# A tile's eight transposes in one PSUM tile of two banks, with one copy, one cast and one subtraction

## The chip, the cores and the metric

The kernel runs on one core of a Trainium2 chip. The metric is the device time of one execution in microseconds. The core has five engines with a queue of instructions each: TensorE (PE in the profile; its weight loads are PEld), ScalarE (ACT), VectorE (DVE), GpSimd (POOL), and SyncE (SP), which here issues all DMAs. Each engine works through its own list in order and waits at an instruction until what that needs is there.

## What is computed

The reference is attention in a window of 64 positions, then two dense layers with an activation between them, twice over (2304 tokens, 512 features):

```
scores = where(mask, (q @ k.T) / sqrt(64), -1e9)        # 4 x 8 heads, 576 positions, head size 64
attn = exp(scores - max); attn = attn / (sum(attn) + 1e-9)
x = (attn @ v), heads side by side                       # 2304 x 512
h = x @ w_in                                             # 512 -> 1024
solu = h * softmax(h)
ln = (solu - mean) / sqrt(var + 1e-6) * g_ln
x2 = ln @ w_out                                          # 1024 -> 512
h = x2 @ w_in2                                           # 512 -> 2048
g = (a0 + a1 h + a2 h^2 + a3 h^3) / (1 + |b0| |h| + |b1| h^2 + 1e-6)
out = g @ w_out2                                         # 2048 -> 512
```

The weights come in double precision, and the products of the dense layers are made of three passes over split operands (high times high, high times low, low times high).

## The kernel before

The 2304 tokens are 18 tiles of 128. The first part of the program takes each tile through attention and the first layer: scores (`s`, L412 and L418), maximum, eight exponentials (`P`, L433), the sum, the normalisation on POOL in two halves (L446), the transposes of the eight 128x128 blocks of `P` (`pt`, L452), their copy to SBUF (`PT`, a helper's line, L316 on ACT or L318 on DVE), attention (`pv`, L472), the copy and the split of its result (`xh`, `xl`), the product with w_in (`h`, L577 for tiles 0 and 1 in plain fp32, L583 to L585 for the others in three passes), maximum, exponential and product of the activation (L591, `e` L595, L600), the layer norm, the transposes of its eight blocks (`pl`, L643), their cast to the high part (`lh`, L316) and the subtraction that gives the low part (`ll`, a helper's line, L312). After every third tile there are four blocks of 24 matmuls with w_out (`x`, L661 to L663). In between, ACT and DVE convert the weights of both layers from double precision (`xi`, `co`, `cc`; L524 to L562), and SP loads them. The second part, from about 300 us on, is the second layer (`hp`, L869 to L871, and `o`, L933 to L935) and has nothing to do with the change.

The transposes go to PSUM tiles of 128x512 fp32, one bank each, from a pool with two buffers under one tag. So one tile's eight transposes are two steps of four (`probs0`, `probs1`; `lnT0`, `lnT1`), each with a copy, or with a cast and a subtraction, of its own; and the four steps of a tile share the two buffers.

What sets the order is a planner (`class Schedule`). Each step is declared with its engine, a duration, the steps that it needs, the buffers that it takes and gives back (`RINGS`), and, for some, a due time (`WANT`). `latest` works due times backwards; `arrange` goes forward in time, and on the engine that is free first takes, of what can start by then, the step with the earliest due time. A table `SHIFT` of over 500 numbers, one for each kind of step, is added to the due times. The program is written out in the order that comes out of this, so each engine's list is fixed when the kernel is built. An h step of a tile needs h's single PSUM buffer, which the product (`solu_mul`, L600) of the tile before gives back.

Of the kernel before, what the change touches and what calls it, by code (L numbers as in the profile page):

```python
# [10 lines left out]
F32 = mybir.dt.float32  # L11
# [17 lines left out]
class Schedule:  # L29
# [131 lines left out]
WANT = {"scores": -14.41, "probs0": -5.07, "probs1": -11.61, "attend": -3.5, "h": 0.0, "lnT0": 18.0, "lnT1": 6.24,  # L161
# [8 lines left out]
    "zeros.0": 1.38, "load_q.0": 6.55, "load_k.0": -28.63, "load_v0.0": 141.12, "load_v1.0": -6.38,  # L170
    "scores.0": -20.87, "max.0": -45.99, "max_scale.0": -4.27, "exp00.0": -66.76, "exp01.0": 3.38, "exp02.0": -5.62,
    "exp03.0": -8.85, "exp10.0": 72.56, "exp11.0": -8.26, "exp12.0": -26.72, "exp13.0": -0.04, "rcp.0": 8.87,
    "norm0.0": 8.54, "norm1.0": 14.81, "probs0.0": 1.34, "probs_copy0.0": -62.03, "probs1.0": -5.85,
    "probs_copy1.0": 18.56, "attend.0": -46.92, "att_hi.0": -12.2, "h0.0": -269.2, "h1.0": 8.67, "h2.0": 3.37,
    "h3.0": 26.22, "solu_max.0": 31.19, "solu_exp.0": 2.85, "solu_mul.0": 11.29, "ln_square.0": -13.95,
    "ln_eps.0": -1.23, "ln_var.0": -50.09, "ln_root.0": 40.62, "ln_newton.0": 40.57, "ln_apply.0": 11.2,
    "lnT0.0": 10.64, "ln_lo0.0": -9.07, "lnT1.0": 26.11, "ln_hi1.0": 49.09, "ln_lo1.0": -7.2, "load_q.1": -15.97,
    "load_k.1": -1.82, "load_v0.1": -24.72, "load_v1.1": -50.83, "scores.1": 25.01, "max_scale.1": 44.65,
    "exp00.1": 3.81, "exp01.1": -10.95, "exp02.1": -8.5, "exp03.1": 0.02, "exp10.1": 44.36, "exp11.1": -14.96,
    "exp12.1": -41.69, "exp13.1": -29.73, "sum.1": -36.73, "rcp.1": 12.45, "norm0.1": -6.86, "norm1.1": -0.75,  # L180
    "probs0.1": -13.21, "probs_copy0.1": -14.32, "probs1.1": 54.09, "attend.1": -31.41, "att_hi.1": 44.51,
    "h0.1": 123.3, "h1.1": -79.07, "h2.1": -8.64, "h3.1": 8.6, "solu_max.1": 1.31, "solu_exp.1": 53.25,
    "solu_mul.1": -102.82, "ln_square.1": -111.94, "ln_eps.1": -5.47, "ln_var.1": 10.19, "ln_root.1": 23.16,
    "ln_newton.1": -19.91, "ln_apply.1": 1.34, "lnT0.1": -250.52, "ln_hi0.1": 42.1, "ln_lo0.1": 3.68,
    "lnT1.1": -90.22, "ln_hi1.1": -0.19, "ln_lo1.1": 0.09, "load_q.2": -53.75, "load_k.2": 2.2, "load_v0.2": 31.73,
    "load_v1.2": 31.01, "scores.2": 4.8, "max.2": 13.85, "max_scale.2": -3.04, "exp00.2": 3.57, "exp01.2": -9.12,
    "exp02.2": -64.47, "exp03.2": -59.28, "exp10.2": 55.78, "exp11.2": -5.48, "exp12.2": -62.63, "exp13.2": 4.22,
    "sum.2": -29.63, "norm0.2": -3.19, "norm1.2": -68.31, "probs0.2": -22.28, "probs_copy0.2": -58.18,
    "probs1.2": 27.82, "probs_copy1.2": 1.45, "attend.2": 54.95, "att_hi.2": 43.76, "att_lo.2": 3.12, "h0.2": 24.95,
    "h1.2": 5.79, "h2.2": 13.56, "h3.2": -33.94, "solu_exp.2": 19.34, "solu_mul.2": 19.14, "ln_square.2": 4.55,  # L190
    "ln_eps.2": -23.38, "ln_var.2": -2.95, "ln_root.2": 253.93, "ln_newton.2": -41.92, "ln_apply.2": -8.79,
    "lnT0.2": 73.62, "ln_hi0.2": 5.39, "ln_lo0.2": 72.68, "lnT1.2": -108.76, "ln_hi1.2": -115.31, "ln_lo1.2": 5.48,
    "x2_0.2": 30.09, "x2_out0.2": 0.27, "x2_1.2": -30.14, "x2_out1.2": -8.97, "x2_2.2": 31.15, "x2_out2.2": -8.93,
    "x2_3.2": -28.94, "x2_out3.2": 9.66, "x2_store.2": 36.3, "load_q.3": 55.5, "load_k.3": -61.69, "load_v0.3": 50.44,
    "load_v1.3": -21.04, "scores.3": 45.91, "max.3": 19.14, "max_scale.3": -27.79, "exp01.3": -57.15,
    "exp02.3": -13.57, "exp03.3": 14.11, "exp10.3": -27.25, "exp11.3": -86.72, "exp12.3": 14.24, "exp13.3": -17.77,
    "sum.3": 16.89, "norm0.3": 67.01, "norm1.3": 10.6, "probs0.3": 48.4, "probs_copy0.3": 14.82, "probs1.3": 46.89,
    "probs_copy1.3": -68.76, "attend.3": -12.43, "att_hi.3": 9.62, "att_lo.3": -2.23, "h0.3": -28.18, "h1.3": 4.45,
    "h2.3": 71.47, "h3.3": -17.32, "solu_max.3": 0.55, "solu_exp.3": -37.61, "solu_mul.3": 7.39,
    "ln_square.3": -13.89, "ln_eps.3": -8.0, "ln_var.3": -24.56, "ln_root.3": -42.0, "ln_newton.3": 18.28,  # L200
    "ln_apply.3": -34.59, "lnT0.3": -21.97, "ln_hi0.3": 2.92, "ln_lo0.3": 53.87, "lnT1.3": -44.68, "ln_hi1.3": 45.82,
    "ln_lo1.3": 55.16, "load_q.4": -0.97, "load_k.4": 79.18, "load_v0.4": 6.74, "load_v1.4": -37.63,
    "scores.4": -50.82, "max.4": -232.11, "max_scale.4": 7.78, "exp00.4": -72.47, "exp01.4": 66.42, "exp02.4": -2.95,
    "exp03.4": -55.86, "exp10.4": -3.36, "exp11.4": -9.42, "exp12.4": 98.46, "exp13.4": -13.13, "sum.4": -2.13,
# [64 lines left out]
FIRST = 2  # L269
# [817 lines left out]
```

## Time and profile before

| | |
|---|---|
| median of 3 runs | 716.35 us (716.21 to 716.68) |
| the profiled execution | 717.4 us, span 715.3 us |
| busy in the span | PE 691.1 us (97%), PEld 612.9 (86%), DVE 575.5 (80%), ACT 488.1 (68%), POOL 89.0 (12%) |
| granted TensorE clock | 1.00 |

The span runs from the first to the last instruction of the profiled execution; what lies around it is 2.1 us. Busy times are shares of the whole span, over parts with different limits. A row of the timeline gives start and duration of an instruction or of several alike merged; where instructions overlap, the distance from start to start (the pitch) is less than the duration. In square brackets stands the engine's idle time ahead of the row, and what ended it.

### The profile page before, as it was taken

Reading aid. Unit: us, or ns where it says so; the run is one execution under the profiler, and the core shown is the slowest. Engines: PE = TensorE matmul, PEld = TensorE weight load, DVE = VectorE, ACT = ScalarE, POOL = GpSimd, SP = SyncE. Lnnn points to the kernel's source line nnn. Section 1 sums busy time; section 2 is a strip of 40 time slices with the busy share of each in tenths; the row PEclk is TensorE's granted clock in tenths of the full one; section 3 lists DMA queues with packets and bytes.
Section 4 is the critical chain, followed back from the end, with each engine's and each line's share of the span. In section 5 each row is a group of like instructions: output and inputs, shape, how many; then the busy total and the mean of one; then the engine's idle time right before and its main releaser. Section 6 shows DMA issues by size and latency. Waiting matters only on the chain.

```text
span 715.3 us, 11585 instructions
## 1 busy us (share of the span) xinstructions
PE 691.1 (97%) x4520; PEld 612.9 (86%) x4520; DVE 575.5 (80%) x713; ACT 488.1 (68%) x918; POOL 89.0 (12%) x142
## 2 busy tenths in 40 slices
PE   2889999999999999999999999999999999999998
PEld 1557899888898899998889988998898889989986
DVE  6899977898999735759998988798598869866973
ACT  6999967768868554748786665766486558555662
POOL 2553332243223220000000000000000000000000
PEclk9999999999999999999999999999999999999999
DMA  9864559668764314426301000200020000001001
GB/s 327 283 218 162 178 202 306 217 215 308 270 231 168 116 45 145 150 68 197 100 22 59 20 1 22 67 1 11 12 68 1 22 30 16 0 1 46 1 0 44
DMA packets 42741, 77.81 MB, mean 109 GB/s; under 512 B 4480, under 2 KB 22912, under 8 KB 42304
## 3 DMA queue, kind: packets, MB, share of 16 engines
q1 hardware_dynamic: 42688, 77.09, 32.1%
q8 instruction: 35, 0.57, 0.3%
q14 instruction: 18, 0.15, 0.1%
HBM read 59.25 MB, written 17.83 MB: 108 GB/s over the span
## 4 chain that ended last, share of the span: by engine, by line
PE 87%; DVE 5%; ACT 4%; DMA 2%; issue 1%; POOL 1%; DVEq 0%; ACTq 0%; POOLq 0%
PE hp L871 8%; PE hp L869 8%; PE hp L870 8%; PE o L935 8%; PE o L934 8%; PE o L933 8%; PE x L661 5%; PE x L663 5%; PE x L662 5%; PE h L583 4%; PE h L584 4%; PE h L585 4%; PE pv L472 3%; PE pl L643 2%; PE pt L452 2%; PE s L418 2%
## 5 line engine op out<-in xcount | busy, mean ns | idle before, releaser
L869 PE MATMUL hp<-x2h,w 128*128 128x384 f32 x384 | 129.4, 337 | 0.7 <-DVE t L902 0.5
L871 PE MATMUL hp<-x2h,w 128*128 128x384 f32 x384 | 129.3, 337 | 0.0
L870 PE MATMUL hp<-x2l,w 128*128 128x384 f32 x384 | 129.2, 337 | 0.0
L935 PE MATMUL o<-w,gl 128*128 128x512 f32 x282 | 111.5, 395 | 0.1
L934 PE MATMUL o<-w,gh 128*128 128x512 f32 x282 | 111.0, 394 | 0.0
L933 PE MATMUL o<-w,gh 128*128 128x512 f32 x282 | 110.7, 393 | 0.0
L879 ACT ACTIVATE w<-hp,ab 128x768 f32<-128x768 f32 x48 | 43.2, 900 | 70.5 <-PE hp L871 70.5
L887 DVE SCALAR_TENSOR_TENSOR w<-r,b,w 128x768 f32<-128x768 f32 x48 | 48.8, 1017 | 37.0 <-ACT r L881 36.9
L869 PEld LDWEIGHTS hp<-x2h,w 128*128 128x128 f32 x384 | 72.1, 188 | 4.0 <-PE hp L871 0.8
L870 PEld LDWEIGHTS hp<-x2l,w 128*128 128x128 f32 x384 | 72.1, 188 | 2.7
L871 PEld LDWEIGHTS hp<-x2h,w 128*128 128x128 f32 x384 | 72.1, 188 | 0.0
L917 ACT CAST gh<-t 128x768 fp32r<-128x768 f32 x48 | 40.1, 835 | 46.8 <-PE o L934 23.8
L661 PE MATMUL x<-lh,wo 128*128 128x384 f32 x192 | 66.7, 348 | 0.0
L663 PE MATMUL x<-lh,wo 128*128 128x384 f32 x192 | 65.0, 339 | 0.0
L662 PE MATMUL x<-ll,wo 128*128 128x384 f32 x192 | 65.0, 338 | 0.0
L935 PEld LDWEIGHTS o<-w,gl 128*128 128x128 f32 x282 | 52.9, 188 | 12.7 <-DVE gl L312 0.5
L934 PEld LDWEIGHTS o<-w,gh 128*128 128x128 f32 x282 | 52.9, 188 | 10.0
L933 PEld LDWEIGHTS o<-w,gh 128*128 128x128 f32 x282 | 53.0, 188 | 9.6
L312 DVE TENSOR_TENSOR gl<-t,gh 128x768 fp32r<-128x768 f32 x48 | 45.8, 954 | 13.8 <-ACT gh L917 13.8
L433 ACT ACTIVATE P<-s,mx 128x128 f32<-128x128 f32 x144 | 52.0, 382 | 2.4 <-POOL mx L428 2.4
L892 ACT ACTIVATE r<-w,qe 128x768 f32<-128x768 f32 x48 | 45.5, 947 | 9.7 <-DVE w L887 9.6
L583 PE MATMUL h<-wi,xh 128*128 128x512 f32 x128 | 50.8, 397 | 0.1
(112 smaller groups left out, 1465.5 us busy)
## 6 DMA issues: line engine op xcount, KB each, us to landing
v<-in_v_dram SPq DMA_DIRECT2D x35, 256.0 KB, 4.1
xc<-in_moe_w_in_dram SPq DMA_DIRECT2D x16, 512.0 KB, 4.4
xc<-in_moe_w_out_dram SPq DMA_DIRECT2D x16, 512.0 KB, 5.4
w2d<-cc SPq DMA_DIRECT2D x16, 512.0 KB, 3.5
r<-w2d SPq DMA_DIRECT2D x16, 512.0 KB, 4.0
k<-in_k_dram SPq DMA_DIRECT2D x17, 384.0 KB, 5.5
q<-in_q_dram SPq DMA_DIRECT2D x18, 256.0 KB, 5.6
x2d<-xs SPq DMA_DIRECT2D x6, 768.0 KB, 4.4
```

What stands on the lines that cost most here:

```text
L433: nc.scalar.activation(Pn[t][:, j, n, :], tiles["s", t][:, j, n, :], AF.Exp, bias=mx[:, c:c + 1], scale=0.125, accum_out=su[:, c:c + 1])
L583: nc.tensor.matmul(o, xh[:, c, :], wh, start=(c == 0), stop=False)
L661: nc.tensor.matmul(o, wh, lh[:, f, :], start=(f == 0), stop=False)
L662: nc.tensor.matmul(o, wh, ll[:, f, :], start=False, stop=False)
L663: nc.tensor.matmul(o, wl, lh[:, f, :], start=False, stop=(f == FC1 - 1))
L869: nc.tensor.matmul(h, wh[:, sl], xh[:, c], start=(c == 0), stop=False)
L870: nc.tensor.matmul(h, wh[:, sl], xl[:, c], start=False, stop=False)
L871: nc.tensor.matmul(h, wl[:, sl], xh[:, c], start=False, stop=(c == KC - 1))
L887: nc.vector.scalar_tensor_tensor(out=w, in0=r, scalar=b1, in1=w, op0=ALU.mult, op1=ALU.add)
L933: nc.tensor.matmul(o, gh[:, n, sl], wh, start=(f == 0), stop=False)
L934: nc.tensor.matmul(o, gh[:, n, sl], wl, start=False, stop=False)
L935: nc.tensor.matmul(o, gl[:, n, sl], wh, start=False, stop=(f == FC2 - 1))
```

## The change

The pool of the transposes has one buffer of 128x1024 fp32, two banks, in place of two of one bank. A tile's eight transposes of `P` are one step (`probs`) with one copy of 128x1024 behind it, and the eight of the layer norm one step (`lnT`) with one cast and one subtraction of that width. The rings change with it: `tr` from 2 to 1, `PT` from four half tiles to two whole ones. `WANT` has one due time for each in place of two. The planner's durations are changed for several other steps (an exponential from 0.36 to 0.37, `e` from 1.25 to 1.34, POOL's normalisation from 1.12 to 1.3, conversions on ACT from 1.06 to 1.16), the whole `SHIFT` table is new, and so the order is another on every engine.

```
-    ptr = ps1.enter_context(tc.tile_pool(name="ptr", bufs=2, space=PSUM))
+    ptr = ps1.enter_context(tc.tile_pool(name="ptr", bufs=1, space=PSUM))
...
-    def probs_T(t, j):
-        pt = ptr.tile([P, NPAIR, P], F32, name=f"pt{t}_{j}", tag="tr")
-        for c in range(NPAIR):
-            nc.tensor.transpose(pt[:, c, :], Pn[t][:, j, c, :], ident)
-        tiles["pt", t, j] = pt
-
-    def probs_copy(t, j, eng):
-        PTs[t, j] = ap.tile([P, NPAIR, P], F32, name=f"PT{t}_{j}", tag="PT", bufs=4)
-        copy(eng, PTs[t, j], tiles["pt", t, j])
+    def probs_T(t):
+        pt = ptr.tile([P, 2, NPAIR, P], F32, name=f"pt{t}", tag="tr")
+        for j in range(2):
+            for c in range(NPAIR):
+                nc.tensor.transpose(pt[:, j, c, :], Pn[t][:, j, c, :], ident)
+        tiles["pt", t] = pt
+
+    def probs_copy(t, eng):
+        PTs[t] = ap.tile([P, 2, NPAIR, P], F32, name=f"PT{t}", tag="PT", bufs=2)
+        copy(eng, PTs[t], tiles["pt", t])
...
+        p = ptr.tile([P, FC1, P], F32, name=f"pl{t}", tag="tr")
+        for f in range(FC1):
+            nc.tensor.transpose(p[:, f, :], tiles["e", t][:, f * P:(f + 1) * P], ident)
...
+        copy(eng, tiles["ln", pr][0][:, :, c * P:(c + 1) * P], tiles["pl", t])
...
+        step("probs", "PE", 0.9, ["norm0", "norm1"], probs_T, t, want=WANT["probs"], take=[("tr", (t, 0)), ("PT", t)],
+             give=[("P", t)])
+        step("probs_copy", "ACT|DVE", (1.03, 1.22), ["probs"], probs_copy, t, give=[("tr", (t, 0))])
...
+        step("lnT", "PE", 0.9, ["ln_apply"] + needs, ln_T, t, want=WANT["lnT"],
+             take=[("tr", (t, 1))] + ([("lnT", pr)] if c0 == 0 else []), give=[("e", t)])
+        step("ln_hi", "ACT|DVE", (1.04, 1.22), ["lnT"], ln_hi, t)
+        step("ln_lo", "DVE", 1.22, ["ln_hi"], ln_lo, t, give=[("tr", (t, 1))])
...
-    "zeros.0": 1.38, "load_q.0": 6.55, "load_k.0": -28.63, "load_v0.0": 141.12, "load_v1.0": -6.38,
```

How instructions move, at three places. In the names, the number at the end tells one buffer's use from the next; line numbers of the new kernel are eight or nine lower.

SP's list at the start of the program, before (xi is w_in of the first layer, k_104 and q_129 belong to tile 0, k_174 and q_171 to tile 1):

```order
L506 DMA xi_102<-in_moe_w_in_dram 128x512 x2
L388 DMA k_104<-in_k_dram 128x4x128
L383 DMA q_129<-in_q_dram 128x512
L506 DMA xi_134<-in_moe_w_in_dram 128x1024
L383 DMA q_171<-in_q_dram 128x512
L390 DMA k_174<-in_k_dram 128x4x192
```

SP's list at the same place now (k_102 and q_125 belong to tile 0, k_179 and q_185 to tile 1, k_167 to tile 2):

```order
L379 DMA k_102<-in_k_dram 128x4x128
L374 DMA q_125<-in_q_dram 128x512
L498 DMA xi_127<-in_moe_w_in_dram 128x512 x2
L498 DMA xi_155<-in_moe_w_in_dram 128x1024
L381 DMA k_167<-in_k_dram 128x4x192
L387 DMA v_0_105<-in_v_dram 64x512
L381 DMA k_179<-in_k_dram 128x4x192
L374 DMA q_185<-in_q_dram 128x512
```

k and q of tile 0 have moved ahead of the first layer's weights; tile 1's wait behind three loads of weights.

ACT's list around the copies of tiles 1 and 2, before (PT_0_416 and PT_1_419 are tile 1's, PT_1_467 and PT_0_469 tile 2's, e_387 is tile 0's):

```order
L316 COPY PT_0_416<-pt_0_374 128x512 [waits PE_49]
L316 COPY PT_1_419<-pt_1_380 128x512 [waits PE_49]
L595 ACTIVATE e_387,st_386<-h_330,st_386 128x1024 [waits DVE_49]
L554 ACTIVATE wo_454<-co_338,gT 128x512 [waits DVE_49,Pool_49]
L316 COPY xh_426<-pv_427 128x512 [waits PE_49]
L316 COPY PT_1_467<-pt_1_449 128x512 [waits PE_49,Activation_49]
L316 COPY PT_0_469<-pt_0_461 128x512 [waits PE_49,Activation_49]
```

ACT's list around the same copies now (PT_369 is tile 1's, PT_462 tile 2's, e_441 tile 0's, P_371 tile 3's):

```order
L307 COPY PT_369<-pt_345 128x1024 [waits PE_49]
L516 ACTIVATE cc_398<-xc_323 128x1024 [waits DMAHW3_49,DMAHW2_49]
L518 ACTIVATE xo_283<-xo_283 128x1024
L307 COPY xh_400<-pv_401 128x512 [waits PE_49]
L424 ACTIVATE P_371,sum_373<-s_375,mx_372 128x128 [waits Activation_49,Pool_49]
L424 ACTIVATE P_371,sum_373<-s_375,mx_372 128x128 x6
L587 ACTIVATE e_441,st_440<-h_275,st_440 128x1024 [waits DVE_49]
L307 COPY PT_462<-pt_445 128x1024 [waits PE_49]
```

Two conversions and seven exponentials of tile 3 have come between the copies of tile 1 and tile 2; tile 0's e stands right ahead of the latter.

DVE's list from the maximum of tile 3's h to its product, before (h_774 and e_844 are tile 3's):

```order
L591 TENSOR_REDUCE st_843<-h_774 128x1 [waits PE_49]
L627 TENSOR_SCALAR st_739<-st_739 128x1 [waits Activation_49]
L628 TENSOR_SCALAR st_739<-st_739 128x1 [waits DVE_49]
L562 SCALAR_TENSOR_TENSOR wo_846<-co_682,gT,wo_846 128x512 [waits Activation_49]
L633 TENSOR_SCALAR e_740<-e_740,st_739 128x1024 [waits DVE_49]
L600 ISA e_844,st_843<-h_774,e_844 128x1024 [waits Activation_49]
```

DVE's list at the same place now (h_815 and e_908 are tile 3's, mx_883 is the maximum of tile 7's scores):

```order
L583 TENSOR_REDUCE st_907<-h_815 128x1 [waits PE_49]
L415 TENSOR_REDUCE mx_883<-s_886 128x8 [waits PE_49]
L521 TENSOR_SCALAR co_878<-co_878 128x1024 [waits Activation_49]
L554 SCALAR_TENSOR_TENSOR wo_873<-co_715,gT,wo_873 128x512
L592 ISA e_908,st_907<-h_815,e_908 128x1024 [waits Activation_49]
```

The layer norm steps of the tile before have left this place, and the maximum of tile 7's scores and a conversion have come in.

## Rows read from the trace of the kernel before

**Rows 1.** Busy time by stretch: stretch, its length, then us of each engine:

```profile
0.00:25.00 25.00, 9.05 (x111) 7.02 (x112) 17.90 (x26) 17.76 (x48) 8.77 (x20) 1.00 0.91 314
25.00:81.00 56.00, 51.90 (x482) 36.33 (x480) 52.66 (x79) 53.32 (x145) 24.34 (x33) 1.00 0.65 216
81.00:320.00 239.00, 239.00 (x1986) 217.96 (x1985) 183.94 (x259) 162.09 (x406) 55.93 (x89) 1.00 0.54 184
```

**Rows 2.** TensorE's waits: us in total, times, longest:

```profile
PE s L412 <- ACT P L433: 6.2, 1, 6.2
...
PE pv L472 <- ACT PT L316: 3.3, 2, 1.9
...
PE pt L452 <- POOL P L446: 2.3, 5, 1.0
```

**Rows 3.** Timeline of TensorE, 139 to 150 us: start, duration:

```profile
139.32 1.03 PE L452 MATMUL pt<-ident,P 128*128 128x128 f32 x8
140.11 0.48 PE L583 MATMUL h<-wi,xh 128*128 128x512 f32 x1
140.43 0.39 PE L584 MATMUL h<-wi,xh 128*128 128x512 f32 x1
...
145.44 0.39 PE L585 MATMUL h<-wi,xl 128*128 128x512 f32 x1
145.76 1.15 PE L472 MATMUL pv<-PT,v 128*64 128x64 f32 x32
...
149.08 0.44 PE L661 MATMUL x<-lh,wo 128*128 128x384 f32 x1
149.36 0.34 PE L662 MATMUL x<-ll,wo 128*128 128x384 f32 x1
149.54 0.34 PE L663 MATMUL x<-lh,wo 128*128 128x384 f32 x1
```

**Rows 4.** Timeline, ACT, DVE and TensorE, pieces between 28 and 64 us:

```profile
28.91 1.21 DVE L312 TENSOR_TENSOR wi<-xi,wi 128x1024 fp32r<-128x1024 f32 x1
30.04 1.22 DVE L536 CUSTOM_DVE_ANT_0 xi<-xi 128x2048 uint16<-128x2048 uint16 x1
...
31.64 1.06 ACT L551 CAST wi<-xi 128x1024 fp32r<-128x1024 f32 x1
32.57 0.39 ACT L433 ACTIVATE P<-s,mx 128x128 f32<-128x128 f32 x1
...
48.44 1.07 ACT L316 CAST lh<-pl 128x512 fp32r<-128x512 f32 x2
49.06 1.29 DVE L312 TENSOR_TENSOR ll<-pl,lh 128x512 fp32r<-128x512 f32 x2
49.38 1.15 ACT L595 ACTIVATE e<-h,st 128x1024 f32<-128x1024 f32 x1
50.27 0.74 DVE L562 SCALAR_TENSOR_TENSOR wo<-co,gT,wo 128x512 fp32r<-128x512 f32 x1
...
63.10 0.66 PE L452 MATMUL pt<-ident,P 128*128 128x128 f32 x4 [0.97 <-POOL P L446]
63.80 0.59 ACT L316 COPY PT<-pt 128x512 f32<-128x512 f32 x1 [0.24 <-PE pt L452]
```

**Rows 5.** Timeline of the head: ACT's first work, then marks of TensorE:

```profile
4.98 0.66 ACT L524 ACTIVATE xi<-xi 128x512 f32<-128x512 f32 x1 [2.98 <-DMA xi<-in_moe_w_in_dram]
...
8.14 1.98 PE L418 MATMUL s<-k,q 64*64 64x128 f32 x32 [3.23 <-DMA q<-in_q_dram]
...
23.44 1.97 PE L472 MATMUL pv<-PT,v 128*64 128x64 f32 x30 [1.90 <-ACT PT L316]
...
27.62 7.96 PE L577 MATMUL h<-xi,xh 128*128 128x512 f32 x16
...
64.89 0.50 PE L583 MATMUL h<-wi,xh 128*128 128x512 f32 x1
...
75.53 0.47 PE L583 MATMUL h<-wi,xh 128*128 128x512 f32 x1
```

## Prediction before the run

> **What bounds the kernel now.** I read the busy time by engine first (the table above: TensorE 97%), then the busy time by stretch, then TensorE's waits, and only then single instructions. By stretch [rows 1] TensorE is idle for 15.95 us before 25 us, for 4.1 us between 25 and 81 us, and for none of the 239 us after that. So from 81 us on the time is the length of TensorE's own list, and only the first 81 us have slack: there ACT is busy for 53.3 and DVE for 52.7 of 56 us, and TensorE's waits name ACT's exponentials, ACT's copies of the transposed probabilities, and POOL's normalisation [rows 2]. A cheaper copy is worth something only there; elsewhere the change can only lose, by making TensorE wait or by lengthening its list.
>
> **TensorE's list.** The transposes themselves are the same 288. Does splitting them into fours cost anything? Eight in a row start at 139.32, the h matmul behind them at 140.11 and the next one at 140.43; the 22 after it, up to 145.44, have a pitch of 0.228 [rows 3]. So 0.79 us plus 0.09 that the first h matmul takes over its usual pitch: 0.88 for eight. That is 0.11 us each with nothing fixed for the block, so 4 + 4 costs what 8 costs: 0. What does cost is a passage between 128-row work and the small-tile work (scores and attention): the h matmul ahead of attention has a pitch of 0.32 for 0.228, the x matmul behind scores 0.28 for 0.18 [rows 3], some 0.2 us for each separate run of small-tile work. The order before has 28 such runs (36 blocks, 8 times two adjacent), the new one 30 (6 times adjacent): 2 x 0.2 = **+0.4 us**. The pieces into which the new order cuts h (six or twelve matmuls) are free by the same rows.
>
> **The copy, the cast and the subtraction.** The mean durations invite the wrong sum: one long instruction for two short ones looks like a gain of a fixed cost each time. But neighbours overlap, so the pitch from start to start counts. Two 512-wide casts start at 48.44 and the next instruction at 49.38: 0.94 us for both; one 1024-wide cast takes 0.93 (31.64 to 32.57) [rows 4]. That one reads SBUF; the trace has no 1024-wide copy out of PSUM, so I bound ACT's gain by 0 and 0.05 us a pair, and take 0.03 (36 pairs: 1.1 us over the kernel). DVE: two subtractions 1.21 us (49.06 to 50.27), one 1024-wide 1.13 (28.91 to 30.04) [rows 4]: 0.08 x 18 = 1.4 us. All but four or five tiles of this lie after 81 us, beside a TensorE that waits for nobody: worth 0 there. In the head it is about 5 x (2 x 0.03 + 0.08) = 0.7 us of two engines that are 94 to 95% busy; it is contained in the walk below.
>
> The Trainium skill ("Perfetto Trace Analysis", Optimizing Scalar/DVE Operations) puts the fixed cost of an instruction on PSUM at about 51 ns for ACT and 125 ns for DVE, and says that profiled durations are about twice the engine's own cost; by it the gain would be 36 x 0.051 = 1.8 us and 18 x 0.125 = 2.3 us of engine time, an estimate, and still beside TensorE for the most part. The same section says that where these engines only cause bubbles on another, breaking instructions up lets work finish sooner, which speaks against this change.
>
> What the one copy adds is delay. Four transposes start at 63.10 and take 0.44 us of list; their copy starts at 63.80 [rows 4], 0.26 us behind. Now that is counted from the fourth transpose, then from the eighth: with halves the second copy ends about 1.75 us after the first transpose starts, with one copy about 0.88 + 0.26 + 1.0 = 2.15: +0.4 us for whoever waits (attention, x, and the next transposes, which now have one buffer and not two).
>
> **The head, walked by hand.** The order is new everywhere, and here it decides. I went along the new lists of PE, ACT, DVE and POOL from one hand-over to the next with pitches as in [rows 4] (1024-wide ACT work 0.93 to 1.1, 1024-wide DVE work 1.13) and the planner's own 0.36 for an exponential, and compare at marks that the trace of before has. No step of it is better than a few tenths.
>
> First mark, attention 0. Before, k and q are loaded behind two pieces of w_in: scores 0 start at 8.14 and attention 0 gets going at 23.44 [rows 5], because the second half's copy has exponentials of tile 1 ahead of it. In the new order k and q are first in SP's queue; the first load before had landed at 4.98 [rows 5], so scores start at about 5.2 and end at 7.2. Reduction, eight exponentials with one conversion between them, normalisation and one copy bring attention 0 to 18.5: a lead of 4.9 us.
>
> Second mark, the end of h of tile 0: before at 27.62 + 7.9 = 35.5 [rows 5]. The new order does h of tile 0 in three pieces, with scores 2 (which wait 1.5 us for tile 1's exponentials), transposes 1, scores 3 and attention 1 between them, and ends it at 36.2. Those last three, some 3.2 us, are then already done: lead 2.5 us.
>
> Third mark. Behind transposes 2, ACT's new list has seven exponentials of tile 3 and then tile 0's e ahead of the copy PT of tile 2. e waits for DVE's maximum of h 0, which ends at 38.5; so e ends at 39.8, the copy at 40.75, and attention 2, next on TensorE, waits from 38.0 to 40.8: 2.8 us. From here a loop rules: h of a tile, maximum (DVE), e (ACT), product (DVE), which frees h's PSUM for the next tile's h. I get h 2 at 55.25 (1.1 us of waiting) and h 3 at 66.3 (1.45 us), where before had 64.89 [rows 5]; but scores 6 and attention 4 (2.3 us) are then done already: lead 0.9.
>
> Fourth mark, h 4: before at 75.53 [rows 5]. In the new order h 3 ends at 71.8. DVE's list from there is maximum 73 to 74.05, scores' maximum 7 (to 75.2), a conversion step, a weight step, product (76.55 to 77.85); ACT does a copy and a conversion ahead of e. TensorE has transposes, scores and attention 5 until 75.95 and waits 1.95 us: h 4 at 77.9, with attention 5 (1.08) ahead. 77.9 - 75.5 - 1.1 = **+1.3 us** behind. After that x of the first three tiles (4.2 us a block) covers the loop, as it does in before from 81 us on. All in all TensorE would be idle for about 9 us after 25 us where it was idle for 4.1, against some 3.5 us saved in the first 25.
>
> **Sum.** +1.3 (head) + 0.4 (passages) = +1.7 us. The profiled execution took 717.4 us, 2.1 around its span and 1.05 above the median of 716.35; since all terms are differences I add them to the median: **718.0 us**. A difference under 0.2% (1.43 us: 714.9 to 717.8) is about what a measurement of this kernel can't tell from none.
>
> **Rivals.** (1) *The lead survives*, faster. If the copy of tile 2 comes before e, or e earlier, the 2.8 us go, and if the loop's waits are no longer than before's, the lead of 2.5 us at the second mark stays: -2.5 + 0.4 gives 714.3. For it: TensorE's start is nearly 5 us earlier beyond doubt, and the planner's durations are now near the trace's (exponential 0.37, e 1.34, POOL 0.5 and 1.3). Against it: the loop's links stand in that order on ACT and DVE, and both engines are 95% busy, so early work displaces other work (a unit of the second layer's weights is converted before 45 us, about 2 us of ACT and 4 of DVE). (2) *No difference that counts*: the walk errs by half its later waits: -0.7 to +1.2, around 716.7. Nothing in the copies pays [rows 4], so only the order is left, and the two orders meet within 1 us at the third mark. (3) *The single buffer binds in the steady stretch*, slower still. At five places a second transpose block follows within 2.5 us of the first (tiles 3 to 6, 16), and in tiles 11 and 12 only six h matmuls (1.37 us) lie between transposes and attention, where 2.15 - 0.79 = 1.36 are needed: no slack, so every ACT instruction of 1 us in front of the copy is 1 us of TensorE. Seven places at 0.4 us: +2.8, 720.8. It decides from the point at which ACT starts copies more than 0.3 us late. Against it: TensorE waited for no one after 81 us under an order made by the same rules. The Trainium skill (same page, Matmuls) says that independent groups should rotate through PSUM banks so that evacuation overlaps the next group; rotation is what the one buffer gives up, and this rival is that rule's result. (4) That the merging does nothing by itself is what [rows 4] say for ACT; it is part of (2).
>
> **Chances.** The forecast (717.8 to 719.3) 0.34, the lead survives 0.20, no difference 0.34, the buffer binds 0.12. Faster by over 0.2%: 0.20; within: 0.36 (the second rival, and a little of the forecast's low side); slower: 0.44. Range: from the first rival to the third, 714.2 to 720.8; by itself the forecast would be 716.7 to 719.5.
>
> **What would show it.** Right: attention 0 starts near 18.5; TensorE's idle time before 25 us falls to about 12.5, and between 25 and 85 us rises to about 9, with waits for PT copies and for the product ahead of h 2 to h 4; h 4 near 78; no wait between 90 and 320 us; one copy of 1024 has a pitch of 0.9 to 0.95. Wrong: idle under 5 us in 25 to 85 us (rival 1), or waits of transposes and attention for ACT's copies and DVE's subtractions after 90 us (rival 3), or a list of TensorE after 90 us that is over 1 us longer or shorter than before's.

## The result and the profile after

| runs | time, median | against before, 95% interval |
|---|---|---|
| before, 3 runs | 716.35 us | |
| after, 3 runs on the same chip | 723.93 us (723.81 to 724.00) | 1.0105 [1.0082, 1.0128] |
| after, 5 runs on another chip (e17) | 722.11 us (721.29 to 722.38) | 1.0072 [1.0060, 1.0084] |

The changed kernel is slower, by 5.2 to 7.6 us. One execution each of e1, e8, e12 and e13 below was far longer (985 us and more); the ratios leave it out, the medians count it, which moves none of them by more than 0.3 us. The profiled execution of after took 724.0 us, its span 722.0 (before 715.3). Busy time by stretch of after, which answers to [rows 1] (stretch, its length, then PE, PEld, DVE, ACT, POOL, and the granted clock as the last but two):

```profile
0.00:25.00 25.00, 9.06 (x116) 6.71 (x116) 16.57 (x23) 14.62 (x39) 7.43 (x20) 1.00 0.86 295
25.00:81.00 56.00, 46.21 (x510) 33.32 (x510) 51.85 (x70) 51.76 (x137) 25.99 (x34) 0.97 0.71 235
81.00:320.00 239.00, 236.48 (x1914) 213.05 (x1911) 181.46 (x250) 163.71 (x382) 54.71 (x89) 1.00 0.53 179
```

TensorE is idle for 15.94 us in the first 25 (before 15.95), for 9.79 us up to 81 (before 4.1) and for 2.5 us after that (before 0). Its waits in after, which answer to [rows 2]:

```profile
PE s L403 <- ACT P L424: 11.5, 3, 7.0
PE h L575 <- DVE st L592: 5.2, 4, 1.7
...
PE pv L464 <- ACT PT L307: 3.5, 2, 2.4
PE s L409 <- DMA q<-in_q_dram: 2.2, 1, 2.2
PE h L569 <- ACT xh L307: 1.4, 1, 1.4
```

The waits for the product ahead of h (L575) are new, and the scores wait for exponentials three times and not once. Of the copies (PT) there are still two waits. The timeline of TensorE in after, which answers to [rows 5]:

```profile
4.70 1.92 PE L409 MATMUL s<-k,q 64*64 64x128 f32 x32
...
16.45 1.99 PE L409 MATMUL s<-k,q 64*64 64x128 f32 x32 [2.17 <-DMA q<-in_q_dram]
...
21.02 1.15 PE L464 MATMUL pv<-PT,v 128*64 128x64 f32 x32 [1.10 <-ACT PT L307]
23.54 1.99 PE L569 MATMUL h<-xi,xh 128*128 128x512 f32 x4 [1.37 <-ACT xh L307]
...
35.74 0.41 PE L403 MATMUL s<-masks,ib 64*64 64x512 bf16 x4 [2.63 <-ACT P L424]
...
37.43 1.97 PE L464 MATMUL pv<-PT,v 128*64 128x64 f32 x32
39.33 2.21 PE L569 MATMUL h<-xi,xh 128*128 128x512 f32 x4
41.47 1.09 PE L444 MATMUL pt<-ident,P 128*128 128x128 f32 x8
45.00 1.15 PE L464 MATMUL pv<-PT,v 128*64 128x64 f32 x32 [2.44 <-ACT PT L307]
...
60.13 0.50 PE L575 MATMUL h<-wi,xh 128*128 128x512 f32 x1 [1.51 <-DVE st L592]
...
78.29 1.04 PE L409 MATMUL s<-k,q 64*64 64x128 f32 x32
...
80.29 1.15 PE L464 MATMUL pv<-PT,v 128*64 128x64 f32 x32
83.10 0.50 PE L575 MATMUL h<-wi,xh 128*128 128x512 f32 x1 [1.65 <-DVE st L592]
...
324.02 0.34 PE L856 MATMUL hp<-x2h,w 128*128 128x384 f32 x1
```

Three more lines of the same timeline before:

```profile
70.56 1.15 PE L472 MATMUL pv<-PT,v 128*64 128x64 f32 x32
...
71.88 1.04 PE L418 MATMUL s<-k,q 64*64 64x128 f32 x32
...
316.66 0.34 PE L869 MATMUL hp<-x2h,w 128*128 128x384 f32 x1
```

Scores 0 start at 4.70 (before 8.14), attention 0 at 21.02 (23.44): the new order leads here by 2.4 us. But tile 4's h starts at 83.10; before it started at 75.53 [rows 5], with one attention (1.08 us) and one tile's scores (1.22) less done by then: attention 5 and scores 7 are through in after (80.29 and 78.29), attention 4 and scores 6 before (70.56 and 71.88). So 83.10 - 75.53 - 1.08 - 1.22 = 5.3 us have been lost ahead of this mark. The last product with w_out ends, and the second part's first long run of hp starts, at 324.02 (before 316.66): 7.4 us, nearly the whole difference of the medians (7.6), lie in the first part. The spans differ by only 6.7, since the second part, which the change leaves alone, took 0.7 us less in this execution than in that of before.

### The profile page after: what moved, and what is told of

Same layout as the page of the kernel before. It is cut to its first block, busy times and chain, and to the rows that moved or that the text cites. A ratio compares the mean times of both kernels' runs of the same rounds, so it can differ in the third digit from the quotient of the medians.

```text
span 722.0 us, 11542 instructions
## 1 busy us (share of the span) xinstructions
PE 689.8 (96%) x4520; PEld 612.4 (85%) x4520; DVE 572.8 (79%) x695; ACT 488.3 (68%) x882; POOL 88.1 (12%) x142
## 4 chain that ended last, share of the span: by engine, by line
PE 85%; DVE 5%; ACT 4%; DMA 4%; POOL 1%; issue 1%; SPq 0%; POOLq 0%; ACTq 0%; DVEq 0%
PE hp L858 9%; PE o L922 9%; PE hp L857 9%; PE hp L856 9%; PE o L921 8%; PE o L920 8%; PE x L652 4%; PE x L654 4%; PE x L653 4%; PE h L575 4%; PE h L576 4%; PE h L577 4%; PE pv L464 2%; PE s L409 2%; PE pt L444 2%; PE pl L634 2%
## 5 line engine op out<-in xcount | busy, mean ns | idle before, releaser
L866 ACT ACTIVATE w<-hp,ab 128x768 f32<-128x768 f32 x48 | 43.2, 900 | 43.6 <-PE hp L858 43.5
L303 DVE TENSOR_TENSOR gl<-t,gh 128x768 fp32r<-128x768 f32 x48 | 45.9, 957 | 28.9 <-ACT gh L904 28.5
L575 PE MATMUL h<-wi,xh 128*128 128x512 f32 x128 | 51.8, 404 | 5.2 <-DVE st L592 5.2
```

The costliest lines, as they stand in the source:

```text
L575: nc.tensor.matmul(o, xh[:, c, :], wh, start=(c == 0), stop=False)
```

## The experiments

The change does two things: it merges two halves into one, and it computes the order anew. The experiments took these apart first. Every time below stands against runs of the kernel before on the same chip (medians 716.6 to 716.9 us).

| label | kernel | median, us | against before, 95% interval |
|---|---|---|---|
| e17 | merged, new order (the changed kernel) | 722.11 | 1.0072 [1.0060, 1.0084] |
| e18 | halves, new order | 722.19 | 1.0072 [1.0058, 1.0085] |
| e1 | halves, new order | 722.31 | 1.0070 [1.0050, 1.0089] |
| e2 | merged, old order | 721.23 | 1.0051 [1.0034, 1.0069] |
| e3 | changed, loads of tile 1 early | 722.22 | 1.0078 [1.0055, 1.0101] |
| e4 | changed, one scaling on VectorE | 722.83 | 1.0079 [1.0054, 1.0104] |
| e5 | changed, spare matmuls in waits | 721.99 | 1.0073 [1.0061, 1.0085] |
| e6 | e3, e4 and e5 together | 722.43 | 1.0084 [1.0069, 1.0099] |
| e7 | e4 with halves | 721.49 | 1.0073 [1.0061, 1.0085] |
| e8 | before, spare matmuls at the start | 715.77 | 0.9987 [0.9978, 0.9996] |
| e9, e10, e11 | changed, tile 0's gate moved up | 726.5, 728.3, 726.5 | 1.013 to 1.016 |
| e12 | before, tile 0's h begun earlier | 719.87 | 1.0038 [1.0025, 1.0050] |
| e13, e14, e16 | old head, new rest | 753.9, 754.5, 751.2 | 1.048 to 1.053 |
| e15 | new head, old rest | 731.97 | 1.0209 [1.0190, 1.0228] |

### Merging or order

**e1, e18: the new order, the halves back.**

```diff
-    ptr = ps1.enter_context(tc.tile_pool(name="ptr", bufs=1, space=PSUM))
+    ptr = ps1.enter_context(tc.tile_pool(name="ptr", bufs=2, space=PSUM))
-        copy(eng, PTs[t], tiles["pt", t])
+        for j in range(2):
+            copy(eng, PTs[t][:, j], tiles["pt", t, j])
```

(The same for the transposes, the cast and the subtraction.)

> The new order on every engine, but a tile's transposes go to two one-bank tiles again, each with its own copy, cast and subtraction, issued back to back where the one stood. Order theory (the loss is the new order of the first 85 us, the merging is worth little): 723.2 to 724.6 us, as the changed kernel, ACT busy about 1 us longer. Merging theory (one buffer and later copies make the loss): 717 to 719.

Measured: 722.31. Against the first three runs of after that looked like 1.6 us for merging and 5 for the order. But these were runs on different chips, and by halves (e7) the kernel of e4 came out level with e4 (1.0073 and 1.0079). So both were run again, side by side, at the end:

> The changed kernel as it is, beside the halves on one chip. Theory (merging costs 1.6 us under the new order): 723.5 to 724.2, and 1.2 to 2.5 us above the run beside it. Rival (the changed kernel's own time is nearer 722.5, and the repairs of its head gave little): 722 to 722.8, within 0.7 us of the run beside it.

> The halves in the new order once more. Theory: 721.7 to 722.5, and in its trace the wait of attention 2 for its copy is 0.5 to 1.3 us shorter than the changed kernel's 2.44, while the waits ahead of the h of tiles 2 to 4 stay at 1.4 to 1.7 us. Rival (halves give back nothing): within 0.7 us of the run beside it.

Measured: 722.11 and 722.19. The rival of both holds: under the new order merging costs and gives nothing that can be measured, to within about 1 us. (The theory of e18 had its time and its waits right too; a gain over e17 it doesn't show.) The timeline of TensorE in e18:

```profile
23.75 3.78 PE L570 MATMUL h<-xi,xh 128*128 128x512 f32 x4 [0.68 <-ACT xh L307]
...
35.98 0.41 PE L403 MATMUL s<-masks,ib 64*64 64x512 bf16 x4 [2.31 <-ACT P L424]
...
38.27 1.98 PE L570 MATMUL h<-xi,xh 128*128 128x512 f32 x4
41.23 1.09 PE L444 MATMUL pt<-ident,P 128*128 128x128 f32 x8 [0.98 <-POOL P L437]
43.52 0.33 PE L465 MATMUL pv<-PT,v 128*64 128x64 f32 x2 [1.20 <-ACT PT L307]
44.01 1.15 PE L465 MATMUL pv<-PT,v 128*64 128x64 f32 x30 [0.16 <-ACT PT L307]
...
82.13 0.50 PE L576 MATMUL h<-wi,xh 128*128 128x512 f32 x1 [1.66 <-DVE st L593]
```

The wait of attention 2 for its copy is shorter, 1.20 + 0.16 and not 2.44, but transposes 2 now wait 0.98 for the normalisation: 2.34 in all. The waits of 2.3 us ahead of scores 3 and of 1.5 us ahead of h are there with halves as well. They belong to the order. (The halves stand here side by side at the place of the merged step; an order of their own they did not have.)

**e2: the old order, merged.** The one transposition, copy, cast and subtraction stand where the later half stood; two transpositions had to go behind a copy for the single buffer to come free.

```diff
+        for t in range(18):
+            for name in ("probs", "probs_copy", "lnT", "ln_hi", "ln_lo"):
+                order.pop(min(at((name + "0", t)), at((name + "1", t))))
...
+                    move(key, freed)
```

> The order of the kernel before on every engine, but the two half steps are one, at the place of the later half: one PSUM tile of two banks, one copy, one cast, one subtraction. Only the layer norm's transposes of tiles 5 and 8 had to move, behind the copies of tiles 7 and 11. Order theory: 715.5 to 718, with some waiting of TensorE where copies now come later. Merging theory: 720 or more.

Measured: 721.23, the rival. Here merging does cost, some 3.7 us by the ratio (4.5 by the medians). TensorE's waits in e2, then two places of its timeline:

```profile
PE pv L509 <- ACT PT L352: 3.9, 2, 2.7
...
PE pl L679 <- ACT PT L352: 2.2, 2, 1.1
```

```profile
120.29 1.03 PE L489 MATMUL pt<-ident,P 128*128 128x128 f32 x8
122.42 1.09 PE L679 MATMUL pl<-ident,e 128*128 128x128 f32 x8 [1.10 <-ACT PT L352]
```

In an order made for two buffers the next transpositions come right behind the first; with one buffer they wait for its copy, in the steady stretch too (at 122.42 and again at 177.78: these are the two that had to be moved, of the layer norm of tiles 5 and 8). The new order keeps them apart: e17 shows no wait of TensorE between 90 and 320 us. Whether its worse head is the price of that was not shown. The Trainium skill says that independent groups should rotate through PSUM banks so that evacuation overlaps the next group ("Perfetto Trace Analysis", Matmuls); e2's 1.10 us agree with it; e17 shows that an order can be found in which it doesn't bind.

### Repairs of the new head

**e3, e4, e5, e6, e7.** Each takes away one thing that the trace of after names in the first 40 us.

```diff
# e3
+        move(("load_k", 1), ("load_q", 0))
+        move(("load_q", 1), ("load_k", 1))
# e4
+        move(("max_scale", 2), ("max", 2), "DVE")
# e5
+            nc.tensor.matmul(spare[:, 0:P], ident, ident, start=True, stop=True)
```

> The changed kernel with one thing moved: k and q of tile 1 are loaded right behind k and q of tile 0, ahead of w_in's. Load theory: tile 1's scores no longer wait until 16.4 us for q and no longer hold up the transposes of tile 0 behind them on TensorE; attention 0 starts near 19 instead of 21.0, and the gain stays: 721.9. Rival (the weights' conversions, now loaded 2 us later, are what the rest waits for): 723.5 to 725.

> The changed kernel with one thing moved: the scaling of the maximum of tile 2 (128x8) is done by DVE right behind the maximum, not by POOL, where it took 1.69 us. Scale theory: exponentials 2 start at 31.2 instead of 32.8, TensorE's wait ahead of scores 3 falls from 2.6 to 1 us, and the clock, granted at half from 36.3 to 39.6 us behind that wait, stays at full: 1.65 + 1.7 us, 720.6. If the clock falls all the same: 722.2. If something else is late next: 723.5 to 724.2.

> The changed kernel with 15 extra 128x128 matmuls on TensorE whose result nothing reads: 5 behind the attention of tile 0, 10 behind the transposes of tile 1, the two places where its trace shows TensorE waiting (1.37 us at 23.54, 2.63 us at 35.74). Theory (the clock's fall is part of the loss): with the engine kept at work in these waits the granted clock stays at 1.00 from 20 to 45 us, scores 3 take 1.04 again and not 1.54, attention 1 1.15 and not 1.97, and the time is 1.7 us shorter, 722.2. Rival (the fall costs nothing, since another engine is late anyway): 723.9. Rival (the spares themselves hold scores 3 up): above 724.3.

> The changed kernel with three repairs of its head at once: k and q of tile 1 loaded behind those of tile 0, the scaling of tile 2's maxima on VectorE, and spare matmuls in the two waits (5 and 4). Theory (three separate terms of the head that add): their single gains of 1.7, 1.1 and an expected 1.7 us give 719.4. Rival (they lie one behind the other, so that where one is taken away the next is late): as good as the best of them alone, 721.5 to 722.2. If the whole loss lay in the head as the walk has it, 718.0.

> The changed kernel with its halves back (two one-bank tiles, two copies, casts and subtractions each, in the new order) and the scaling of tile 2's maxima on VectorE. Theory (merging and head are separate terms): 723.9 - 1.6 - 1.1 = 721.2; the waits for the product ahead of the gates of tiles 2 to 4 stay at 1.4 to 1.7 us each, and the wait of attention 2 for its copy is 0.5 to 1 us shorter. Rival (merging is what makes these waits): they fall to under 0.8 us each and the time to 719 or less.

Measured: all five between 721.5 and 722.8, and each interval overlaps that of e17. Each edit did what it says; none gave time back that can be measured against e17. In the expectations I had taken 723.9 for the changed kernel on these chips, so the gains of "1.7" and "1.1" in them were no gains. Why e3 gives nothing is seen in its timeline:

```profile
15.37 1.97 PE L420 MATMUL s<-k,q 64*64 64x128 f32 x32
17.27 2.14 PE L455 MATMUL pt<-ident,P 128*128 128x128 f32 x8
20.51 1.15 PE L475 MATMUL pv<-PT,v 128*64 128x64 f32 x32 [1.10 <-ACT PT L318]
24.53 3.78 PE L580 MATMUL h<-xi,xh 128*128 128x512 f32 x4 [2.87 <-ACT xh L318]
```

The wait for q is gone and attention 0 is 0.5 us earlier, but the copy of its output comes 1 us later: the weights' first piece is converted from 9.69 and not 8.30, since two more loads are ahead of it, and on ACT that copy stands behind a cast which waits 1.4 us for VectorE's part of the conversion. In e4 scores 3 begin at 34.87 (after 35.74) and tile 4's h at 81.64, 1.3 us ahead of e17's 82.93; but this trace is of its fastest execution (721.27; the others 721.86 to 724.53), so that is no gain of the kernel.

In e5 and e6 the spare matmuls fill the waits, and the clock stays up there; it falls at another place (from 43 us on in e5, between 30 and 36 us in e6). The busy time of e5 by stretch:

```profile
36.00:42.00 6.00, 5.02 (x80) 3.46 (x76) 5.29 (x8) 6.00 (x19) 4.19 (x5) 1.00 0.56 183
...
44.00:47.00 3.00, 3.00 (x52) 2.69 (x56) 2.78 (x6) 3.00 (x7) 1.79 (x3) 0.50 0.96 352
```

### Moving the gate

**e9, e10, e11.** If the end of tile 0's h (41.5 us in after, 35.5 before) sets the loop's start, bringing it forward should give the time back.

```diff
+        move(("h3", 0), ("probs", 1))
+        move(("solu_max", 0), ("rcp", 2))
+        move(("solu_exp", 0), ("max", 3))
+        move(("solu_mul", 0), ("solu_exp", 0))
# e10, e11
+            ahead((f"h{n}", 1), ("attend", 2))
```

> The changed kernel with the last quarter of tile 0's h taken out from behind scores 3 and attention 1 and put right behind the transposes of tile 1, and the three steps of its gate (maximum, exponential, product) moved up with it on VectorE and ScalarE. Theory (the end of tile 0's h is the mark from which the loop counts): it ends at 38 to 38.5 us in the place of 41.5, since its weights' last operation ends at 36.2; attention 2 and scores 4 still stand ahead of tile 1's h, so that starts at 45.5 to 46.5 in the place of 47.29, and the time is about 1 us shorter than the changed kernel: 722.9. Rival (the mark doesn't matter): 723.9 or more, with scores 3 and tile 3 later by 1 to 2 us.

> As the kernel before this one, and tile 1's h put ahead of attention 2 and scores 4, as the kernel before the change has it. Theory: tile 1's h starts at 42 to 43.5 us in the place of 47.29, the waits for the copy of tile 2 (2.44 us) vanish behind it, tile 4's h starts 3 to 4 us earlier than 83.1, and the time is 720 (719 to 721). Rival (the loop is bound behind it by the single two-bank buffer and the product, whenever it begins): tile 4's h within 1 us of 83.1 and 723.

> The same order, with the halves back (two one-bank tiles, copies, casts and subtractions each by half). Theory (merging itself costs 1.6 to 2 us, by a start of the copies half a passage later): 1.6 us below the run beside it, about 718.4. Rival (what merging cost was the wait ahead of tile 1's h, which is gone here): the same as the run beside it, within 0.7 us.

In all three the last quarter of tile 0's h multiplies weights whose conversion still has two operations to go, so tile 0's h is not the right product; and VectorE waits 1.6, 1.7 and 3.3 us for these matmuls before it goes on with the conversion. So they measure more than the move. Measured: 726.5, 728.3 and 726.5. e9 falls to its rival, the other two are slower than both of theirs. (e11's median is 1.9 us below e10's, which is the difference that its theory had for merging; but its executions go from 724.9 to 730.0, the intervals overlap, and its wait on VectorE is another.) The timelines of TensorE and of VectorE in e10:

```profile
42.74 1.97 PE L463 MATMUL pt<-ident,P 128*128 128x128 f32 x8 [3.60 <-POOL P L456]
44.50 7.68 PE L588 MATMUL h<-xi,xh 128*128 128x512 f32 x16
...
59.52 0.64 PE L422 MATMUL s<-masks,ib 64*64 64x512 bf16 x4 [4.03 <-ACT P L443]
```

```profile
36.06 1.22 DVE L544 SCALAR_TENSOR_TENSOR xi<-xi 128x1024 uint32<-128x1024 uint32 x1 [1.72 <-PE h L588]
...
38.94 0.19 DVE L452 RECIPROCAL rc<-rc 128x8 f32<-128x8 f32 x1
```

Tile 0's h ends at 36.0 and tile 1's starts at 44.5 (after 47.29; expected were 42 to 43.5). But transposes 2 wait 3.6 us for the normalisation, and scores 5, which follow scores 4 at 53.2 where after had them at 46.1, wait 4.0 us for exponentials 4. Tile 2's h starts at 65.6 (after 60.13). So an early gate alone did not help: the chain of scores, exponentials and normalisation from tile to tile came later. How far the move itself did that is not shown, for part of it is VectorE's wait: the reciprocal of tile 2, which the normalisation needs, stands behind it and starts at 38.94 (after 36.32), 1.0 us after its input was there.

**e12: the kernel before, tile 0's h begun earlier.**

```diff
+        move(("probs1", 0), ("probs0", 0))
+        move(("probs_copy1", 0), ("probs_copy0", 0))
+        ahead(("attend", 0), third)
+        ahead(("att_hi", 0), third)
+        move(("h0", 0), ("att_hi", 0))
```

> The kernel before, with its halves and its own order but for three moves at the start: the two copies of tile 0 one right behind the other on ScalarE, attention 0 behind them, its output's copy ahead of the last three exponentials of tile 1, and the first quarter of tile 0's h ahead of scores 2. Theory (the end of tile 0's h is the mark): attention 0 starts at 21.8 and not 23.4, the h of tile 0 ends at 33.8 to 34.5 and not 35.6, and the time is 1 to 1.5 us shorter than the kernel before: 715.4. Rival (behind it the normalisation of tile 2's probabilities is late, which ends at 39.9 us): the same, 716.7. Rival (scores 2 one us later delay tile 2): 717.7.

Measured: 719.87, the third case and more. Attention 0 started at 21.76 and h at 25.02 (27.62 before), but scores 2 at 28.39 (25.34 before), tile 0's h ended at 35.1 (35.4 before, expected 33.8 to 34.5), and tile 4's h started at 76.86 (75.53 before). The gate hardly moved, and the scores of the next tile were held up by 3 us: a step that is moved up delays those that it is put ahead of. The trace is of an execution of 718.2 us; where the rest of the median's loss lies it doesn't show.

### Crossing heads and rests

**e13 to e16.** Steps up to one tile's h in one kernel's order, the later ones in the other's.

```diff
+        there = {k for k, _ in HEAD}
+        order = HEAD + [o for o in order if o[0] not in there]
```

> Halves; every step up to tile 4's h in the order of the kernel before, all later ones in the order of the changed kernel. Theory (the order's 5 us are lost ahead of tile 4's h): like the kernel before, 716.7, and not below 715.0. Rival (the new order loses behind it): 719 or more.

> Merged; order as in the run beside it (the kernel before's up to tile 4's h, the changed kernel's behind). Theory (merging costs by its waits in the head, since behind it the new order was made for one buffer): 1.5 to 2.5 us above the run beside it, 718.2 to 719.2, and 2 to 3 us below the merged kernel in the old order throughout (721.2). Rival (merging needs the new order in the head as well): 721 or more. Rival (merging costs nothing in a good head): within 0.7 us of the run beside it.

> Halves; every step up to tile 3's h in the order of the changed kernel, all later ones in the order of the kernel before. Theory (the order's loss is in its head): 5 us above the kernel before, 721.7 (720.7 to 722.7). Rival (the loss is the head and the rest not fitting, or comes behind tile 4): 717 to 719.

> As e13, with 18 extra matmuls on TensorE whose result nothing reads, 6 ahead of the scores of tile 0 and 12 behind them. Theory (as in the kernel before, where they gave 0.9 us): 0.5 to 1 us below e13. Rival (noise): the same as e13 within 0.4 us.

Measured: 732 to 754. None of the expected times; crossing the orders costs 15 to 38 us. e14 is level with e13, and e16 some 2.5 us below it, with intervals that overlap. The largest of TensorE's waits in e13:

```profile
PE pt L542 <- DVE ll L401: 14.0, 2, 9.3
```

They come long after tile 4's h (they end at 113.47 and 159.15). VectorE is not overloaded there: between 88 and 200 us it waits 28.5 us for conversions on ACT, and these wait 23.7 us for stores and 8.4 for a load of weights. That points to transfers of weights which the crossed lists no longer fit. These four say nothing on where the order loses. That rests on the marks of the traces.

**e8: the kernel before, spare matmuls at the start.**

```diff
+        order.insert(at(("scores", 0)), (("fill", 6), "PE"))
+        order.insert(at(("scores", 0)) + 1, (("fill", 12), "PE"))
```

> The kernel before with 18 extra 128x128 matmuls on TensorE whose result nothing reads: 6 ahead of the scores of tile 0, 12 behind them, in waits of 3.23 and 6.18 us. Theory (the half pace of the first 28 us is a matter of TensorE's idling and lies on the path): scores 1, transposes 0, attention 0 and scores 2 take 1.04 to 1.15 us each and not 1.92 to 2.11, attention 0 starts 0.5 to 1 us earlier, and the time is 1 to 2.5 us shorter than the kernel before. Rival (the conversions on VectorE and ScalarE set the head): the passages are shorter, the time the same within 0.5 us. Rival (the pace has nothing to do with idling): passages as before, time the same or up to 1 us longer.

Measured: 715.77, 0.13% [0.04, 0.22] below the kernel before, between the theory and its first rival. Only scores 0 are shorter (1.10 us for 1.98); scores 1, transposes 0, attention 0 and scores 2 take 1.92 to 2.11 us as before, so the theory of the half pace was tested on one passage only. It is the fastest kernel of this study, by less than the 0.2% that can be told with confidence. Tile 4's h starts at 75.10 (75.53 before).

## Why the prediction was wrong

It said 718.0, slower rather than faster, by the order and not by the copies. The cause held (e17 and e18: the order, and not the merging), the size did not: 722.1 to 723.9, outside the range (714.2 to 720.8). The direction held too, but by luck, as the count at the fourth mark shows.

**The copies: right.** One copy of 1024 in after, on ACT:

```profile
43.95 1.00 ACT L307 COPY PT<-pt 128x1024 f32<-128x1024 f32 x1
44.84 0.38 ACT L424 ACTIVATE P<-s,mx 128x128 f32<-128x128 f32 x1
```

Its pitch is 0.89 us, 0.05 less than that of two 512-wide ones [rows 4], the upper end of the bound. That it is worth nothing measurable in the whole is e17 against e18.

**TensorE's list: +0.4 was right.** From tile 4's h to the long run of hp behind the last product with w_out, less the attention and the scores that the new order has done ahead of it (2.30), before takes 316.66 - 75.53 - 2.30 = 238.8 us, and e8 the same (316.21 - 75.10 - 2.30). The new order takes 322.24 - 82.93 = 239.3 in e17 and 321.86 - 82.13 = 239.7 in e18: 0.5 to 0.9 us longer. The whole spans can't show such a term, since the second part behind it took from 397.3 us (e18) to 398.6 (before).

**The head: the step that failed, +1.3.** The walk against the traces, start or end in us:

| mark | walk | after | e17 | e18 (halves) |
|---|---|---|---|---|
| attention 0 | 18.5 | 21.02 | 20.82 | 21.11 |
| end of tile 0's h | 36.2 | 41.5 | 41.4 | 40.3 |
| attention 2 | 40.8 | 45.00 | 44.85 | 44.01 |
| tile 2's h | 55.25 | 60.13 | 59.98 | 59.14 |
| tile 3's h | 66.3 | 71.47 | 71.34 | 70.54 |
| tile 4's h | 77.9 | 83.10 | 82.93 | 82.13 |

By the second mark the walk is 4.1 to 5.3 us ahead of the traces, and it stays 3.2 to 5.2 ahead of them. The steps from there on were right: the wait of 2.8 us for the copy of tile 2 is 2.44, and from tile 2's h to tile 4's it is 22.97 us where the walk had 22.65. The error lies ahead of the end of tile 0's h, where walk and trace part in three places:

1. *Attention 0, 2.5 us.* ACT's and POOL's first work in after:

```profile
8.30 0.66 ACT L516 ACTIVATE xi<-xi 128x512 f32<-128x512 f32 x1 [6.31 <-DMA xi<-in_moe_w_in_dram]
...
10.18 0.34 ACT L424 ACTIVATE P<-s,mx 128x128 f32<-128x128 f32 x1
```

```profile
14.40 2.48 POOL L437 TENSOR_TENSOR P<-P,rc 128x512 f32<-128x512 f32 x2 [0.32 <-DVE rc L433]
```

With k and q loaded first, w_in lands 3.3 us later than before ([rows 5]: 4.98). Three conversions of it stand ahead of the exponentials of tile 0, which begin at 10.18 although scores 0 end at 6.6 (7.2 in the walk). Then the normalised P of tile 0 is there at 16.88, but on TensorE scores 1 stand ahead of its transposes and wait for q of tile 1, a wait that the walk doesn't have and gives no reason to leave out: they start at 16.45 and take 1.99 us, so the transposes start at 18.37. By the walk's own 2.15 us from the transposes to attention they would have started at 18.5 - 2.15 = 16.35.

2. *POOL's scaling of the maxima, 1.2 us.* The prediction calls the planner's durations near the trace's, with 0.5 us for this operation. In after, and in the kernel before:

```profile
31.07 1.69 POOL L419 TENSOR_SCALAR mx<-mx 128x8 f32<-128x8 f32 x1 [0.33 <-DVE mx L415]
```

```profile
20.03 1.69 POOL L428 TENSOR_SCALAR mx<-mx 128x8 f32<-128x8 f32 x1
```

The trace of before had the number; I hadn't looked. So exponentials 2 start at 32.80 and scores 3 wait 2.63 us.

3. *The clock, up to 1.7 us.* Behind that wait the passages from 36 to 40 us run at half pace (below): attention 1 takes 1.97 us and not 1.15, the last quarter of h 2.2.

Which of the three carries the lag is not shown: e3, e4 and e5 each take one of them away and e6 all three, and none is faster beyond its interval.

**The count at the fourth mark: a slip the other way.** The walk lets TensorE do transposes, scores and attention 5 ahead of tile 4's h, but takes only attention 5 (1.08) off as done ahead. The scores, those of tile 7, are done ahead as well, as the lines of the result show; at the third mark the walk had counted both (2.3). By its own marks the walk gives 77.9 - 75.53 - 2.30 = +0.1 and not +1.3, and the sum 716.35 + 0.1 + 0.4 = 716.9, no difference that counts. That the forecast lay on the slower side came from this slip.

So the head was +5.3 us in after, 5.1 in e17 and 4.3 in e18, in place of +1.3. With the list it is 5.1 + 0.5 = 5.6 in e17 and 4.3 + 0.9 = 5.2 in e18, against 5.5 and 5.6 by the medians. The first three runs had 2 us more. In their trace tile 4's h is 0.2 us later than in e17, and 1.2 us more go between 128 and 142 us, where a wait for a product accounts for 0.58 (135.87; e17 has none there), and 0.4 between 181 and 198; the rest I can't place.

**"Some 3.5 us saved in the first 25" did not happen.** Idle before 25 us is 15.94, forecast 12.5; idle from 25 to 85 us is 9.79 + 1.65, forecast 9. The walk's lead of 4.9 us at attention 0 was 2.4.

**The rivals.** The lead did not survive (1). No difference (2) did not hold either, though it is what the walk gives when it is counted right. The single buffer bound nothing in the steady stretch of the new order (3): e17 has no wait there; the mechanism is real, as e2 shows, but this order avoids it. That the merging does nothing by itself (4) is right under the new order, and wrong under the old.

**What stays open.** Which single thing would mend the new head: none of the five repairs did, and the crossed orders lost more at and behind their seams. The traces tell where the time is lost, and e17 and e18 that the order loses it. What made the order worse was not tested: the ring of one buffer, the planner's new durations and the new table came together, and no order for two buffers was made with the latter two. That some order for one buffer has a head as good as before's wasn't shown either way.

## What to carry to other kernels

An edit that comes with a recomputed order is two changes, and the order may be the larger one: run the old form in the new order and the new form in the old order before any time is put down to the edit. A walk through a new order is only as good as its first marks, so take each duration from the trace, at that place and beside those neighbours, and ask of every load which others now stand ahead of it. Where two orders are compared at a mark, count every kind of work done by then on both sides. Compare repairs with the changed kernel on the same chip; a first difference of 2 us between chips made two repairs look good that were not.

## What the runs showed of the hardware

**TensorE's granted clock falls behind waits, in most heads and not always at the same place.** After's granted clock by microsecond (the column after POOL):

```profile
35.00:36.00 1.00, 0.26 (x8) 0.26 (x11) 1.00 (x2) 1.00 (x5) 0.23 (x1) 1.00 0.13 51
36.00:37.00 1.00, 1.00 (x32) 1.00 (x29) 0.39 (x2) 1.00 (x2) 0.61 (x2) 0.70 0.01 2
37.00:38.00 1.00, 1.00 (x21) 0.67 (x16) 0.44 (x1) 1.00 (x2) 0.72 (x1) 0.50 0.08 16
```

0.50 is the level of 1.2 GHz. The engine had waited 2.63 us up to 35.74. In e3 the fall is at 23 to 29 us, in e4 at 23 to 27, in e5 at 43 to 47, in e2 at 66 to 70, each behind a wait or two; e17 has two, e18 none.

**The column says 1.00 at the start, the instructions say otherwise.** In before 32 score matmuls take 1.98 us at 8.14 [rows 5] and 1.04 later. In e18 four h matmuls take 3.78 us at 23.75 and 1.98 at 38.27, the column at 1.00 throughout. With spare matmuls in the first waits (e8) the scores at 8.09 take 1.10 us, so the pace hung on what TensorE had done before; behind the next wait of 4.2 us the low one is back, and now the column shows it. The busy time of e8 by stretch:

```profile
14.00:16.00 2.00, 0.00 (x0) 0.00 (x0) 0.96 (x2) 2.00 (x9) 0.00 (x0) 0.71 0.98 406
16.00:20.00 4.00, 3.39 (x41) 2.62 (x40) 3.21 (x5) 3.22 (x5) 3.34 (x4) 0.50 0.89 216
```

**VectorE and GpSimd hold each other up.** A scaling of 128x8 on GpSimd takes 0.25 us alone (8.02 in after) and 1.69 beside VectorE (31.07); the VectorE operation beside GpSimd's normalisation of tile 0, at 14.66, takes 1.33 us, elsewhere 0.69. The Trainium skill ("SBUF — State Buffer", Who interferes with whom) says that the two share a pair of ports under an exclusive lock, and that the one that comes second waits until the first is done; here 31.07 lies inside a VectorE operation with two inputs from 30.90 to 32.11, which agrees in that the scaling waits; it ends at 32.76, only behind VectorE's next operation too (32.04 to 32.72).
